# Batches 5 and 6 of a fused cross attention and SiLU network: the fourth half product in seven quarter products, with copies moved to ScalarE and an add moved on GpSimd

## Chip, cores and metric

One NeuronCore of a Trainium2 chip runs the kernel. The metric is the device time of one execution in microseconds (us); lower is better. Engines are named as in the profile: PE is TensorE (matrix products), PEld its weight loads, DVE is VectorE, ACT is ScalarE, POOL is GpSimd, SP is the queue of SyncE, which here issues most DMA transfers.

## What is computed

For each of 8 batches and 8 heads, x (512 tokens of 64) reads from a state of 32 rows by softmax attention, and the state reads from x. Both results are put side by side (544 rows a batch, 512 wide) and go through a two-layer network with SiLU.

```python
def _attn_ref(x, state):                      # x [8, 8, 512, 64], state [8, 8, 32, 64]
    scores = scale * np.matmul(x, state.transpose(0, 1, 3, 2))
    a = softmax(scores)
    xread = np.matmul(a, state)
    scores2 = scale * np.matmul(state, x.transpose(0, 1, 3, 2))
    a2 = softmax(scores2)
    sread = np.matmul(a2, x)
    return np.concatenate([xread, sread], axis=2)

def _moe_ref(x, w_in, w_out):                 # [4352, 512], [512, 2048], [2048, 512]
    h = x @ w_in
    g = h * (1.0 / (1.0 + np.exp(-h)))
    return g @ w_out
```

## The kernel before

**The tiling.** The tokens of a batch are one unit. For xread, `W1 = state @ w_in` is formed per batch in pieces of 512 columns (`w1_mms` on PE into PSUM, `w1_out` copying to bf16), so that h is `aT` times `W1`: `emit_G1(k)` does one block of 128 of the 2048 columns (L566, two matmuls of 128x512) and ScalarE applies SiLU (L594). The result g of a batch is kept in two tiles, `lo` (blocks 0 to 7) and `hi` (8 to 15). A ninth "batch" (number `B` = 8) is sread of all batches, with four matmuls a block (L584) from `xmT`.

**The second layer** is a product of 512 tokens by 2048 by 512, done from batch 1 on by a Strassen-Winograd scheme: seven half products (`Unit.mm(p, k)`, p from 1 to 7, L764), each of 256 tokens by 1024 by 256, that is 8 steps k of two matmuls of 128x256, in place of eight. Their operands are sums of parts of g (`sums1` to `sums4`, on VectorE) and of w_out (`D1` to `D4`). Two accumulators in PSUM are used: `al` (tag o1) collects products 1, 6 and 5, `be` (tag o0) takes 7, 2, 4 and 3 one after the other. What has to outlive an accumulator is copied to `kept[0]` (after product 1), `kept[1]` (product 7) or straight to the output tile (`keep`, after 6 and after 5).

**A half product in quarters.** `Split` does a half product by the same scheme once more: seven quarter products of four matmuls of 128x128 (L689), in the order 1, 2, 4, 7, 6, 3, 5. Its left sums are four VectorE operations (`sums`), its right sums `inner_weights`. Quarters 1, 6 and 5 add into one accumulator `o_ch`, in one of the four banks a0 to a3 that are handed out in turn by `bank`; the others have columns of `be`. VectorE copies `o_ch` to `kept` after 1 and again after 6, adds after 3, and copies and adds after 5. Before the change product 7 is so done in batches 2 to 7, and products 4 (`p4`) and 3 (`p3`) in batch 7.

**The order** is written out by hand: each engine does its instructions in the order in which the program issues them, and a semaphore wait stands where data or a buffer is shared. In batch b the loop over j emits the blocks of h of b and, between them, products 1 and 7 (`early`). After it come W1 pieces, scores and sread for later batches (`group_a`, `out_a`), product 2, product 6 (`units(6)`), `keep` on ScalarE, the add of `kept[1]` on GpSimd, product 4 (`units(4)`), further W1 pieces (`group_b`), product 5 and product 3. `units` puts blocks of h of the next batch between the steps where `leads` says so: none in product 4; in batch 7 the blocks of sread stand between the steps of products 6 to 3 (`upto`).

Other names: `exps_t(m)` is the exponential of the scores of batch m = b + 2 (two on ScalarE, with loads of the function table before and after, by the `warm` instructions) and a DMA transpose of it on SP; `norm_t` normalises it (VectorE and GpSimd). `sread_out` scales what the state read (VectorE) and `transpose_xm` transposes it by DMA; `place_xm(half, eng)` copies it into `xmT`, half 0 for batches 0 to 3. `last_weights` makes the right sums that `p4` (i from 0) and `p3` (from 4) need. `out_half` stores an output tile.

Of the kernel before, what the change touches and what calls it, by code (L numbers as in the profile page):

```python
# [9 lines left out]
BF16 = mybir.dt.bfloat16  # L10
# [8 lines left out]
B = 8  # L19
# [23 lines left out]
def kernel(  # L43
# [8 lines left out]
    nc = tc.nc  # L52
    ds = bass.ds
# [419 lines left out]
        for i, b in enumerate(bs):  # L473
            nc.sync.dma_start_transpose(xs[:, b, :], xm[:, i].rearrange("p g d -> p (g d)"))

    def place_xm(half, eng):
        src = xs.rearrange("p b (k o n) -> p b k o n", k=2, o=2)
        for hg in range(2):
            for odd in range(2):
                copy(  # L480
                    eng,
                    xmT[ds(64 * (odd ^ hg), 64), half, ds(2 * hg, 2), :, :],
                    src[ds(64 * hg, 64), ds(4 * half, 4), :, odd, :].rearrange(
                        "p b k n -> p k n b"
                    ),
                )
# [23 lines left out]
    def w1_out(b, cols, engs, pss, at=0):  # L510
        for f, n in cols:
            for hg in range(2):
                copy(engs[hg], W1[b][:, hg, ds(f + at, n)], pss[f, hg][:, ds(at, n)])
# [105 lines left out]
    def add(eng, dst, a, c):  # L619
        eng.tensor_tensor(dst, a, c, op=ADD)  # L620
# [29 lines left out]
    INNER = (2, 3, 4, 5, 6, 7)  # L650

    class Split:
        def __init__(self, unit, left, right, t, d, kept):
            self.unit, self.t, self.d, self.kept = unit, t, d, kept
            self.x, self.y = quarters(left), quarters(right)
            self.chain = None
            self.begun = set()
# [68 lines left out]
    class Unit:  # L726
# [53 lines left out]
                self.s2 = spool.tile([128, 8, 256], BF16, tag="s2", name="s2")  # L780
            sub(nc.vector, self.s2[:, k], self.hi[:, k, 256:512], self.lo[:, k, 256:512])

        def sums1(self):
            self.s1 = spool.tile([128, 8, 256], BF16, tag="s1", name="s1")
            for k0 in (0, 4):
                k = ds(k0, 4)
                add(nc.vector, self.s1[:, k], self.s2[:, k], self.lo[:, k, 0:256])

# [5 lines left out]
        def inner_sums(self, which):  # L794
            if self.inner is None:
                t = spool.tile([128, 4, 4, 128], BF16, tag="s1", name="inner")
                self.inner = Split(self, self.lo[:, :, ds(256, 256)], D3, t, wt2, self.kept[1])
            self.inner.sums(which)

        def block(self, i, c):  # L800
# [220 lines left out]
    def last_weights(i0, k):  # L1021
        for i in range(i0, i0 + k):
            w, d = divmod(i, 4)
            inner_weights(d, nc.vector, last_d[:, w], (D4, B22)[w])
# [6 lines left out]
    for b in range(1, B):  # L1031
# [2 lines left out]
        u = Unit(b)  # L1034
        lead = LEADS.get(b, 5)
        inner = b in INNER
        if b == 2:
            todo = [(1, k - 8, k + 4) for k in range(5)] + [(7, 1, 9)]
            todo += [(7, 2, 10), (7, 4, 10), (7, 7, 11), (7, 6, 12), (7, 3, 12), (7, 5, 13)]
            todo += [(1, k - 8, (k + 23) // 2) for k in range(5, 8)]  # L1040
        elif inner:
            todo = [(1, k - 8, k + 2) for k in range(6)] + [(7, 1, 9)]
            todo += [(7, 2, 10), (7, 4, 10), (7, 7, 11), (7, 6, 12), (7, 3, 13), (7, 5, 14)]
            todo += [(1, k - 8, 15) for k in (6, 7)]
        else:
            last = 6
            todo = [(1, k - 8, k + 2) for k in range(last)]
            todo += [(7, k - 8, k + 4) for k in range(8)]
            todo += [(1, k - 8, k + 2) for k in range(last, 8)]
        n_todo = len(todo)  # L1050

        def unit():
            p, k, _ = todo.pop(0)
            if k > 0:
                u.inner.mm(k)
                return
            u.mm(p, k + 8)
            if k == -1:
                copy(
                    nc.vector,  # L1060
                    u.kept[int(p == 7)][:],
                    (u.al if p == 1 else u.be)[:],
                )
# [9 lines left out]
        for j in range(lead, NFT):  # L1073
            upto(NFT * b + j + 1)
            if j == 8:
                u.hi = gh[b, 1]
            if j == max(lead, 5):
                u.sums3(0, 4)
                if b == 1:
                    transpose_x(3)  # L1080
                    for v in range(2):
                        evict_state(v, (nc.vector, nc.gpsimd)[v], 2, 2)
                if inner:
                    u.inner_sums((3,))
                if n > B - 2:
                    last_weights(4 * (n - B + 1), 2)
                if 1 < b and m + 1 < B:
                    fetch_x(m + 1)
            if j == 9:
                u.sums3(4, 4)  # L1090
                if inner:
                    u.inner_sums((1, 2, 4))
                if b == 1:
                    for i in range(4):
                        inner_weights(i, nc.vector)
                    spread_x(2)
                    for v in range(2):
                        evict_state(v, nc.gpsimd, 4, 4)
            if n > B - 2 and j == 12:
                last_weights(4 * (n - B + 1) + 2, 2)  # L1100
            early(j)
            if j == 13:
                u.sums2(0, 4)
                if b == 1:
                    fetch_x(4)
# [8 lines left out]

        def out_a():
            i, cols, engs, pss = made[0][0]
            w1_out(i, cols, (nc.scalar, nc.scalar) if b == 1 else engs, pss)
            xm = sread_out(srs, made[1]) if srs and m < B else None
            for piece in made[0][1:]:
                w1_out(*piece)  # L1120
            return xm

        while todo:
# [6 lines left out]
            u.sums1()  # L1130
        if 2 < b < B - 1:
            xm = out_a()
        if n == B:
            upto(NFT * B + 2)
            p4 = Split(u, u.hi[:, :, 256:512], D4, last_t[:, 0], last_d[:, 0], u.kept[0])
            p4.sums((3, 1, 2, 4))
        if b == 1:
            for hg in range(2):
                scores(2, hg)
# [5 lines left out]
            made = group_a()  # L1145
        add(nc.vector, u.block(0, 0), u.kept[0][:], u.be[:])
        if b > 1:
            u.sums1()
        if m == B:
            xm = sread_out(srs, made[1])  # L1150
        if b == 1:
            for hg in range(2):
                exps(2, hg)
# [2 lines left out]

        if b == 2:
            out_a()
        if 1 < b and m < B:
            exps_t(m)  # L1160
        if m == B:
            transpose_xm(srs, xm)
# [2 lines left out]
        def units(p, leads={}, split=None, into=None):  # L1165
            nonlocal step
            for k in range(8 if split is None else 7):
                if split is None:
                    u.mm(p, k)
                else:  # L1170
                    split.mm(ORDER[k], into)
                if n == B and (p != 6 or k > 5):
                    upto(NFT * B + 3 + (step + 1) * (NFT - 3) // 24)
                    step += 1
                    if (p, k) == (3, 1):
                        sread_diff()
                if n < B and k in leads:
                    upto(NFT * n + leads[k])

        units(6)  # L1180
        u.keep(nc.scalar, 1, 0)
        if b == 1:
            for hg in range(2):
                norm(2, hg)
        add(nc.gpsimd, u.block(1, 0), u.block(1, 0), u.kept[1][:])
        if b == 1:
            made = group_a()
            for c in range(4):
                cast_x(4, nc.gpsimd, c, 1)
            for hg in range(2):  # L1190
                transpose_a(2, hg)
            exps_t(m)
            transpose_x(4)
            xm = out_a()
        if m < B:
            nc.scalar.activation(warm[:], busy[:, 0:1], func=SILU, bias=0.0)
        if n < B:
            units(4)
            u.sums4()
            add(nc.vector, u.block(1, 0), u.block(1, 0), u.be[:])  # L1200
        else:
            units(4, split=p4)
            u.sums4()
            add(nc.vector, u.block(1, 0), u.block(1, 0), u.kept[0][:])
            p3 = Split(u, u.hi[:, :, 0:256], B22, last_t[:, 1], last_d[:, 1], u.kept[0])
            p3.sums((1, 2, 3, 4))
        def group_b():
            if b in PIECES_B:
                c = PIECES_B[b]
                pss = w1_next(2) + (w1_next(1, new_h) if c == 3 else [])  # L1210
                for i in (2, 0, 1)[3 - c :]:
                    if b == 1 and i == 1:
                        pss[i] = pss[i][:2] + ((nc.vector, nc.vector),) + pss[i][3:]
                    w1_out(*pss[i])

        if b > 1:
# [12 lines left out]
        else:  # L1229
            units(3, split=p3, into=u.block(0, 1))  # L1230
        if m == B:
            for half in range(2):
                place_xm(half, (nc.vector, nc.gpsimd)[half])
        if m < B:
            normed = norm_t(m)
        if n == B - 2:
            last_d, last_t = (
                xfpool.tile([128, 2, 4, 4, 128], BF16, tag=f"x_f{i}", name=nm)
                for i, nm in enumerate(("last_d", "last_t"))
            )  # L1240
# [46 lines left out]
```

## Time and profile before

| | us |
|---|---|
| median of three runs | 199.74 (199.67 to 199.80) |
| the profiled execution | 199.7 |
| its span | 197.9 |
| half products on PE (L764), busy | 46.6 + 27.4 + 14.4 |
| h on PE (L566, L584), busy | 72.8 + 9.4 |
| SiLU on ScalarE (L594), busy | 79.9 |
| GpSimd's adds to the output (L620), busy | 11.3 + 9.2 |

The span runs from the first to the last record of one execution; what lies around it makes up the rest of the time. The granted clock of PE was 0.996 of full speed over the span. Matmuls overlap: one of 128x256 shows 273 ns and one of 128x128 219 ns, from its start until its result is out, though the next one starts long before that. How long a run of matmuls holds PE is therefore read from the start of the run to the start of what follows.

By engine the busy share of the span is 97% on PE, 81% on VectorE, 70% on ScalarE and 37% on GpSimd. Batch 5's products 2 to 5 lie between 132.6 and 139.6 us, batch 6's between 152.8 and 160.5, batch 7's between 173.4 and 184.5; the last product ends at 194 us.

### The profile page before, as it was taken

What the parts mean: (1) busy time and instruction counts of PE and PEld (TensorE: products, weight loads), DVE (VectorE), ACT (ScalarE), POOL (GpSimd) and SP (SyncE); (2) the same over time, 40 slices, a digit from 0 to 9 for tenths busy, and PEclk for the clock granted to TensorE, in tenths of its full rate; (3) what the DMA queues carried; (4) which work ended last, traced back from release to release, by engine and by line L of the source; (5) the groups of instructions that cost most, each with busy time, mean ns of one, the idle gap of its engine ahead of it and who ended that gap; (6) DMA issues with size and microseconds to landing.
All of it is one profiled execution on the core that took longest, in us unless ns stands there. A gap on an engine that the chain in (4) does not pass through costs nothing.

```text
span 197.9 us, 4924 instructions
## 1 busy us (share of the span) xinstructions
PE 191.8 (97%) x2004; PEld 130.4 (66%) x2004; DVE 159.8 (81%) x314; ACT 138.8 (70%) x255; POOL 73.8 (37%) x97
## 2 busy tenths in 40 slices
PE   7899999999999999999999999999999999999992
PEld 2344455467766676667766776668766866699981
DVE  3755678999899799769994979779688998896782
ACT  3875496689779797889788967889588167825530
POOL 8595332895693008500850047102400236002220
PEclk9999999999999999999999999999999999999998
DMA  5999999999359462594239930942090005000043
GB/s 181 216 206 250 258 207 341 263 263 253 70 95 276 104 212 56 185 230 171 53 133 204 250 61 4 294 92 53 3 267 3 3 13 212 3 2 0 22 193 106
DMA packets 40838, 28.75 MB, mean 145 GB/s; under 512 B 27248, under 2 KB 37488, under 8 KB 40816
## 3 DMA queue, kind: packets, MB, share of 16 engines
q1 hardware_dynamic: 34736, 20.58, 39.8%
q0 software_dynamic: 5792, 7.60, 18.4%
q8 instruction: 15, 0.25, 0.5%
q10 hardware_dynamic: 288, 0.26, 0.4%
q14 instruction: 7, 0.06, 0.1%
HBM read 17.43 MB, written 8.91 MB: 133 GB/s over the span
## 4 chain that ended last, share of the span: by engine, by line
PE 94%; DMA 2%; DVE 1%; POOL 1%; ACT 0%; issue 0%; POOLq 0%
PE o L764 37%; PE h L566 28%; PE ps_w L499 4%; PE o L603 4%; PE o L689 4%; PE h L584 4%; PE o_a L603 3%; PE o_ch L689 3%; DMA x_f<-in_x_dram 2%; PE o_s L830 2%; PE o L830 1%; PE ps_sr L438 1%; PE ps_xt L261 1%; PE ps_at L420 1%; PE ps_sc L318 1%; PE ps_scT L344 1%
## 5 line engine op out<-in xcount | busy, mean ns | idle before, releaser
L594 ACT ACTIVATE g<-h 128x512 bf16<-128x512 f32 (+1 forms) x142 | 79.9, 573 | 29.0 <-PE h L566 17.5
L566 PE MATMUL h<-aT,W 128*128 128x512 bf16 x252 | 72.8, 379 | 0.0
L764 PEld LDWEIGHTS <-g 128*128 128x128 bf16 x432 | 41.7, 98 | 20.7 <-DVE kept L620 0.7
L764 PE MATMUL o<-w_out_sb,g 128*128 128x256 bf16 x320 | 46.6, 273 | 0.0
L620 POOL TENSOR_TENSOR o_sb<-o_sb,kept 128x512 f32<-128x512 f32 (+1 forms) x8 | 11.3, 1418 | 76.9 <-ACT o_sb L166 64.5
L566 PEld LDWEIGHTS <-W 128*128 128x128 bf16 x252 | 23.1, 98 | 7.0 <-issue 0.6
L764 PE MATMUL o<-wt,s 128*128 128x256 bf16 x224 | 27.4, 273 | 0.0
L168 DVE CAST W<-ps_w 128x512 bf16<-128x512 f32 (+1 forms) x34 | 21.2, 665 | 4.8 <-PE ps_w L499 4.8
L764 PEld LDWEIGHTS <-s 128*128 128x128 bf16 x224 | 21.5, 98 | 4.5 <-issue 2.1
L166 ACT ACTIVATE W<-ps_w 128x512 bf16<-128x512 f32 (+1 forms) x32 | 16.8, 582 | 7.5 <-PE ps_w L499 7.5
L168 POOL CAST x_nat<-x_f 128x512 bf16<-128x512 f32 x24 | 16.5, 728 | 3.3 <-DMA x_f<-in_x_dram 3.3
L166 ACT ACTIVATE o_sb<-o 128x512 f32<-128x512 f32 x15 | 8.9, 595 | 8.9 <-PE o L764 4.5
L620 POOL TENSOR_TENSOR o_sb<-kept,o_sb 128x512 f32<-128x512 f32 x7 | 9.2, 1307 | 15.3 <-ACT o_sb L166 15.3
L617 DVE TENSOR_TENSOR g<-g 128x1024 bf16<-128x1024 bf16 x15 | 10.8, 718 | 4.5 <-ACT g L594 4.5
L764 PE MATMUL o<-wt,g 128*128 128x256 bf16 x112 | 14.4, 273 | 0.0
L617 DVE TENSOR_TENSOR g<-g,s 128x1024 bf16<-128x1024 bf16 x14 | 14.2, 1058 | 0.0
L620 DVE TENSOR_TENSOR o_sb<-o_sb,o 128x512 f32<-128x512 f32 (+1 forms) x13 | 8.6, 661 | 3.6 <-PE o L764 2.0
L617 DVE TENSOR_TENSOR s<-g 128x512 bf16<-128x512 bf16 (+3 forms) x23 | 11.4, 523 | 0.0
L689 PEld LDWEIGHTS <-inner 128*128 128x128 bf16 x96 | 7.3, 98 | 5.4
L168 DVE COPY kept<-o_ch 128x128 f32<-128x128 f32 x16 | 4.6, 288 | 7.0 <-PE o_ch L689 6.9
L499 PE MATMUL ps_w<-w_in_sb,stT 64*32 64x512 bf16 (+1 forms) x264 | 10.2, 375 | 0.0
L603 PEld LDWEIGHTS <-g 128*128 128x128 bf16 x64 | 5.6, 98 | 6.4 <-issue 1.1
(143 smaller groups left out, 284.2 us busy)
## 6 DMA issues: line engine op xcount, KB each, us to landing
out_dram<-o_sb SPq DMA_DIRECT2D x14, 512.0 KB, 2.8
x_f<-in_x_dram SPq DMA_DIRECT2D x6, 512.0 KB, 4.5
w_out_sb<-in_moe_w_out_dram POOLq DMA_DIRECT2D x8, 256.0 KB, 9.8
x_f<-in_x_dram POOLq DMA_DIRECT2D x2, 1024.0 KB, 11.6
x_f<-in_x_dram SPq DMA_DIRECT2D x2, 1024.0 KB, 6.3
w_in_sb<-in_moe_w_in_dram POOLq DMA_DIRECT2D x3, 512.0 KB, 10.0
x_f<-in_x_dram POOLq DMA_DIRECT2D x2, 512.0 KB, 10.3
out_dram<-o_sb SPq DMA_DIRECT2D x4, 256.0 KB, 5.0
```

The source lines that it names most:

```text
L166: nc.scalar.activation(dst, src, func=COPY, bias=0.0)
L168: eng.tensor_copy(dst, src)
L499: nc.tensor.matmul(pss[f, hg][ds(32 * s, 32), 0:n], stT[ds(r, 64), b, h // 2, s % 2, :], w_in_sb[ds(r, 64), h // 2, ds(f, n)], start=True, ...
L566: nc.tensor.matmul(h_ps[k][:], W1[b][:, hg, ds(128 * ft, 128)], aT[b][:, hg, :, :], start=(hg == 0), stop=(hg == 1), skip_group_check=True,)
L584: nc.tensor.matmul(ps[:, 0:256], w_in_sb[:, kt, ds(128 * ft, 128)], xmT[:, :, kt].rearrange("p t n b -> p t (n b)"), start=(kt == 0), stop ...
L594: nc.scalar.activation(gt[k], ps[:, 0:n], func=SILU, bias=0.0)
L603: nc.tensor.matmul(outs[tt][:], gt[b * NFT + ft][:, ds(128 * tt, 128)], w_out_sb[:, ft, :], start=(ft == 0), stop=(ft == NFT - 1), skip_gr ...
L617: eng.tensor_tensor(dst, a, c, op=SUB)
L620: eng.tensor_tensor(dst, a, c, op=ADD)
L689: nc.tensor.matmul(to, left[:, k], right[:, k], start=where not in self.begun, stop=(k == 3), skip_group_check=True,)
L764: nc.tensor.matmul(to[:, t, :], left[:, ds(128 * t, 128)], right[:, k, :], start=first and t == 0, stop=(k == 7), skip_group_check=True,)
L830: nc.tensor.matmul(to[:, 0:n], left[:, k], right[:, k, ds(c, n)], start=(first and k == 0), stop=(k == 7), skip_group_check=True,)
```

## The change

In batches 5, 6 and 7 (`split`) product 4 is done in quarters; before, in batch 7 alone. Around it:

- `last_weights` runs in batches 5 and 6 (before: 6 and 7), and its tiles are taken after batch 4 (before: 5).
- In batches 5 and 6 ScalarE copies product 1 to `kept[0]` (before: VectorE).
- In batches 5 and 6 ScalarE does all copies of the W1 pieces of `out_a` (before: VectorE and ScalarE, half each). In `group_b` of batch 6 ScalarE copies the first piece, which now lies in the tag h1 of PSUM, and VectorE the second.
- `sread_out` of batch 6 comes ahead of product 2 (before: after it).
- In batches 5 to 7 `sums1` is cut in two: the second half is issued after the first quarter of product 4.
- In batch 5 `exps_t` comes after `keep` (before: ahead of product 6).
- In batches 2 to 7 GpSimd's add of `kept[1]` comes after VectorE's add of product 4 (before: ahead of product 4).
- `place_xm(0)` moves from the end of batch 6 into the loop of batch 7, in two parts.

```diff
-    def place_xm(half, eng):
+    def place_xm(half, eng, hgs=(0, 1)):
         src = xs.rearrange("p b (k o n) -> p b k o n", k=2, o=2)
-        for hg in range(2):
+        for hg in hgs:
...
-        def sums1(self):
-            self.s1 = spool.tile([128, 8, 256], BF16, tag="s1", name="s1")
-            for k0 in (0, 4):
+        def sums1(self, ks=(0, 4)):
+            if ks[0] == 0:
+                self.s1 = spool.tile([128, 8, 256], BF16, tag="s1", name="s1")
+            for k0 in ks:
...
+        split = b in (5, 6, 7)
...
                 copy(
-                    nc.vector,
+                    nc.scalar if b in (5, 6) else nc.vector,
                     u.kept[int(p == 7)][:],
...
-                if n > B - 2:
-                    last_weights(4 * (n - B + 1), 2)
+                if b in (5, 6):
+                    last_weights(4 * (b - 5), 2)
+                if n == B:
+                    place_xm(0, nc.vector, (0,))
...
-            if n > B - 2 and j == 12:
-                last_weights(4 * (n - B + 1) + 2, 2)
+            if b in (5, 6) and j == 12:
+                last_weights(4 * (b - 5) + 2, 2)
+            if n == B and j == 12:
+                place_xm(0, nc.vector, (1,))
...
-            w1_out(i, cols, (nc.scalar, nc.scalar) if b == 1 else engs, pss)
+            w1_out(i, cols, (nc.scalar, nc.scalar) if b == 1 or split else engs, pss)
             xm = sread_out(srs, made[1]) if srs and m < B else None
-            for piece in made[0][1:]:
-                w1_out(*piece)
+            for i, cols, engs, pss in made[0][1:]:
+                w1_out(i, cols, (nc.scalar, nc.scalar) if split else engs, pss)
...
+        if m == B:
+            xm = sread_out(srs, made[1])
+        if split:
+            p4 = Split(u.hi[:, :, 256:512], D4, last_t[:, 0], last_d[:, 0], u.kept[0])
+            p4.sums((3, 1, 2, 4))
         if n == B:
             upto(NFT * B + 2)
-            p4 = Split(u, u.hi[:, :, 256:512], D4, last_t[:, 0], last_d[:, 0], u.kept[0])
-            p4.sums((3, 1, 2, 4))
...
         if b > 1:
-            u.sums1()
-        if m == B:
-            xm = sread_out(srs, made[1])
+            u.sums1((0,) if split else (0, 4))
...
-        if 1 < b and m < B:
+        if 1 < b < 5:
             exps_t(m)
...
                     split.mm(ORDER[k], into)
+                    if (p, k) == (4, 0):
+                        u.sums1((4,))
...
         u.keep(nc.scalar, 1, 0)
+        if b == 5:
+            exps_t(m)
...
-        add(nc.gpsimd, u.block(1, 0), u.block(1, 0), u.kept[1][:])
         if b == 1:
+            add(nc.gpsimd, u.block(1, 0), u.block(1, 0), u.kept[1][:])
...
-        if n < B:
+        if split:
+            units(4, split=p4)
+            u.sums4()
+            add(nc.vector, u.block(1, 0), u.block(1, 0), u.kept[0][:])
+        else:
             units(4)
             u.sums4()
             add(nc.vector, u.block(1, 0), u.block(1, 0), u.be[:])
-        else:
-            units(4, split=p4)
-            u.sums4()
-            add(nc.vector, u.block(1, 0), u.block(1, 0), u.kept[0][:])
-            p3 = Split(u, u.hi[:, :, 0:256], B22, last_t[:, 1], last_d[:, 1], u.kept[0])
+        if b > 1:
+            add(nc.gpsimd, u.block(1, 0), u.block(1, 0), u.kept[1][:])
+        if n == B:
+            p3 = Split(u.hi[:, :, 0:256], B22, last_t[:, 1], last_d[:, 1], u.kept[0])
             p3.sums((1, 2, 3, 4))
...
-                pss = w1_next(2) + (w1_next(1, new_h) if c == 3 else [])
+                if m == B:
+                    pss = w1_next(1, new_h) + w1_next(1)
+                else:
+                    pss = w1_next(2) + w1_next(1, new_h)
                 for i in (2, 0, 1)[3 - c :]:
-                    if b == 1 and i == 1:
-                        pss[i] = pss[i][:2] + ((nc.vector, nc.vector),) + pss[i][3:]
+                    if b == 1 and i == 1 or m == B:
+                        eng = nc.scalar if m == B and i == 0 else nc.vector
+                        pss[i] = pss[i][:2] + ((eng, eng),) + pss[i][3:]
...
         if m == B:
-            for half in range(2):
-                place_xm(half, (nc.vector, nc.gpsimd)[half])
+            place_xm(1, nc.gpsimd)
...
-        if n == B - 2:
+        if b == 4:
             last_d, last_t = (
```

More of the change, by code (lines that the diff above doesn't have):

```diff
@@ L652, with __init__ @@
     class Split:
-        def __init__(self, unit, left, right, t, d, kept):
-            self.unit, self.t, self.d, self.kept = unit, t, d, kept
+        def __init__(self, left, right, t, d, kept):
+            self.t, self.d, self.kept = t, d, kept
             self.x, self.y = quarters(left), quarters(right)
@@ L796, in inner_sums @@
                 t = spool.tile([128, 4, 4, 128], BF16, tag="s1", name="inner")
-                self.inner = Split(self, self.lo[:, :, ds(256, 256)], D3, t, wt2, self.kept[1])
+                self.inner = Split(self.lo[:, :, ds(256, 256)], D3, t, wt2, self.kept[1])
             self.inner.sums(which)
```

## The prediction

> **What bounds the kernel now.** I read the busy times first, then the chain of waits, then the timelines of the engines around the fourth product in batches 5, 6 and 7. Busy time and chain:
>
> ```profile
> PE 191.8 (97%) x2004; PEld 130.4 (66%) x2004; DVE 159.8 (81%) x314; ACT 138.8 (70%) x255; POOL 73.8 (37%) x97
> ...
> PE 94%; DMA 2%; DVE 1%; POOL 1%; ACT 0%; issue 0%; POOLq 0%
> ```
>
> The end is set by TensorE (PE), which from about 17 us to the last product at 194 us is never idle. So what the other engines are spared is worth nothing by itself; only TensorE's own work and any wait that is put into its stream count. TensorE's timeline, batch 5 before (columns: start, length, then the instructions run together):
>
> ```profile
> 136.10 1.91 PE L764 MATMUL o<-wt,g 128*128 128x256 bf16 x16
> 137.85 1.91 PE L764 MATMUL o<-wt,s 128*128 128x256 bf16 x16
> ```
>
> These are the fourth and the fifth half product. From start to start a whole half product takes 137.85 − 136.10 = 1.75 us. Batch 7 already does its fourth product in quarters (in the order 1, 2, 4, 7, 6, 3, 5), with h products (L584) between:
>
> ```profile
> 177.72 0.39 PE L689 MATMUL o_ch<-wt,g 128*128 128x128 bf16 x4
> 177.94 0.39 PE L689 MATMUL o<-wt,g 128*128 128x128 bf16 x4
> 178.16 0.60 PE L584 MATMUL h<-xmT,w_in_sb 128*128 128x256 bf16 x4
> 178.60 0.39 PE L689 MATMUL o<-last_d,g 128*128 128x128 bf16 x4
> 178.82 0.39 PE L689 MATMUL o<-last_d,last_t 128*128 128x128 bf16 x4
> 179.04 0.60 PE L584 MATMUL h<-xmT,w_in_sb 128*128 128x256 bf16 x4
> 179.48 0.39 PE L689 MATMUL o_ch<-last_d,last_t 128*128 128x128 bf16 x4
> 179.71 0.39 PE L689 MATMUL o<-wt,last_t 128*128 128x128 bf16 x4
> 179.93 0.60 PE L584 MATMUL h<-xmT,w_in_sb 128*128 128x256 bf16 x4
> 180.37 0.39 PE L689 MATMUL o_ch<-last_d,last_t 128*128 128x128 bf16 x4
> ```
>
> **The quarters.** Without the h products the seven cost 0.44 + 0.44 + 0.45 + 0.22 (to 180.59) = 1.55 us, 28 matmuls of 55 ns. Each split thus takes 0.20 us of work off TensorE, and the two of batches 5 and 6 together 0.40 us. This is the whole gain that the change can have.
>
> **The wait that comes with them.** Products 1, 6 and 5 add into one accumulator, o_ch, which VectorE copies away after 1 and after 6; product 5 may not touch it until the copy after 6 is done. VectorE's timeline of the same batch 7 product:
>
> ```profile
> 179.91 0.29 DVE L168 COPY kept<-o_ch 128x128 f32<-128x128 f32 x1 [1.48 <-PE o_ch L689]
> 180.30 0.74 DVE L620 TENSOR_TENSOR kept<-kept,o 128x256 f32<-128x256 f32 x2
> ```
>
> Product 6 starts at 179.48 and is out at 179.87 (its 0.39), the copy begins 0.04 later and takes 0.29. To hand the accumulator back costs about 0.06 (the first transposed x was copied until 6.58, and TensorE went on at 6.64). That is 0.78 us from the start of 6 to the start of 5. In batch 7 it is covered: 6, 3 and an h product take 0.89. In batches 5 and 6 `units(4, split=p4)` has no leads, so nothing but product 3 lies between, and 6 and 3 take 0.44. TensorE waits 0.78 − 0.44 = 0.34 us in each batch, if VectorE is free when 6 ends. It is not quite: the second half of sums1 is now queued behind the copy after 1. Counted from the start of the fourth product, that copy runs from 0.43 to 0.71, the half sum (1.29/2 = 0.65) to about 1.36, while 6, begun at 0.89, is out at 1.28. That adds about 0.05 (0 to 0.15). The copy after 1 itself is done at 0.77 with its handing back, before 6 wants it at 0.89: no wait there.
>
> So the fourth product takes 1.55 + 0.34 + 0.05 = 1.94 us against 1.75: **+0.19 in each batch, +0.38 together**; bounds 1.89 to 2.05, so +0.28 to +0.60. What is queued behind the wait is everything on TensorE, the fifth product first.
>
> **Is the rest ready in time?** In batch 5's clock of before:
> - VectorE loses the copy of the first product (0.68) and two W1 casts (1.28) and gains four sums (1.6, as the same four in batch 7 from 174.34 to 175.93). It adds block(0,0) at about 134.65, as before at 134.80, does half of sums1 and is free at 135.95; the copy after product 1 is due at 136.53. In batch 6 sread_out comes ahead (0.17 + 0.42), and it is free some 0.4 us before. No wait.
> - ScalarE in batch 5: copy of the first product to 132.8, four W1 copies of 0.54 to 135.0, the table load (1.28) to 136.3, keep to 137.1. The fifth product needs the keep at 137.85 or later: 0.7 us of cover. Then two exps (1.15), a load (1.28), ready at 139.5, where the next h is out at 140.2 before: 0.7 us. The exps' transpose is issued some 2 us later, and norm_t with it; its aT is wanted a batch later, at 160.5.
> - After the split VectorE still has two adds, a copy and an add (1.45 as from 180.30 to 181.70), then sums4, the first half about 139.8; the third product starts past 140.2. Cover 0.4 us, thinner than before. This works because GpSimd's add has left sums4:
>
> ```profile
> 136.60 2.36 DVE L617 TENSOR_TENSOR g<-g,s 128x1024 bf16<-128x1024 bf16 x2
> ...
> 137.03 1.38 POOL L620 TENSOR_TENSOR o_sb<-o_sb,kept 128x512 f32<-128x512 f32 x1 [12.74 <-ACT o_sb L166]
> ...
> 181.62 1.28 DVE L617 TENSOR_TENSOR g<-g,s 128x1024 bf16<-128x1024 bf16 x2
> ```
>
> The same pair of sums takes 2.36 us beside that add (first two lines, batch 5) and 1.28 alone (last line, batch 7). The move saves VectorE 1.1 us in batches 2 to 6, worth nothing on the path. GpSimd's casts of x, block(1,1), its half of norm_t and SP's stores queue behind the add and start 1 to 2 us later in batches 2 to 5; what they feed is due most of a batch later. Zero, bounds −0.05 to +0.1 for all of them.
>
> **Batch 7** has half of xmT's placing moved into it, in place of last_weights (which batches 5 and 6 take on, with room as in batch 6 before). VectorE there:
>
> ```profile
> 169.63 0.41 DVE L617 TENSOR_TENSOR last_d<-w_out_sb 128x512 bf16<-128x512 bf16 x1
> 169.96 0.42 DVE L617 TENSOR_TENSOR last_d<-w_out_sb,last_d 128x512 bf16<-128x512 bf16 x1
> 170.50 0.29 DVE L168 COPY kept<-o_ch 128x128 f32<-128x128 f32 x1
> ```
>
> Two copies of 0.64 (four took 2.56 in batch 6) replace this pair of 0.75, +0.5 us; the earlier pair ran 1.2 us beside GpSimd's copies, and its successor takes 1.3 to 1.7. VectorE is 0.55 to 1.0 late at the copy after inner product 6: it ends at 171.2 to 171.6 with the handing back at 171.3 to 171.7, where product 5 is due at 171.38. Loss 0 to 0.3, and I take 0.1. GpSimd's add also comes later, beside the sums of p3 from 183.43 on. At the row for such a sum beside GpSimd (0.73 against 0.42) they end near 185.9 instead of 184.98, and the copy near 186.2, just before its product 6 at 186.28: nothing, or up to 0.2 if it slips.
>
> The Trainium skill, SBUF — State Buffer, section Who interferes with whom, says more: a VectorE operation with two inputs from SBUF and a GpSimd operation that reads SBUF lock each other out for a whole instruction. By it this slip would be up to one GpSimd add, some 1.3 us minus the slack, though the rows above show both engines working on, stretched.
>
> **Sum.** 0.38 + 0.1 = +0.48 us. The profiled execution is 199.7 (span 197.9 and 1.8 around it), the median 199.74: 199.74 + 0.48 = **200.2 us**.
>
> **Rivals.**
> 1. *Batch 7 becomes VectorE's*: the upper bounds there, +0.3 at 171 us and +0.2 at 186 us on top of 0.38, so 200.6. For it: VectorE has no gap between 171.15 and 177.8. Against: 0.36 us of idle time before the adds at 171.15 takes up part.
> 2. *The wait is mostly covered*: VectorE turns the copy round in 0.6 instead of 0.78, and both batches come out even with the 0.20 saved. 199.8. Against: 0.39 and 0.29 are rows.
> 3. *Product 5 does not wait*: the faster side, one mechanism at one place. If the hand-over of o_ch from 6 to 5 takes less than 0.44 us, all 0.40 is kept: 199.3. It decides from there on down; each 0.1 above takes 0.2 away over the two batches. Against: the matmul's 0.39 alone nearly fills it.
> 4. *Weights bind in a run of 28.* Weight loads are hidden in the runs so far; if each showed its whole 98 ns, 28 would take 2.74 us, +1.0 per batch: 201.7. Against: 16 in a row at 193.07 take 1.06 with the last one's drain of 0.22, or 56 ns apiece.
>
> The Trainium skill (TensorE: Matmul & The Clock Gate, Back-to-back issue gap) has such a rule against the change: matmuls of 128 columns, each with its own weight load, are sustained at about 81 ns. By it the quarters would take an estimated 28 × 0.081 = 2.27 us, more than the half product they replace; the run of 16 disagrees.
>
> **Chances.** Forecast (199.95 to 200.45) 0.52; rival 1 0.18; rival 2 0.13; rival 3 0.12; rival 4 0.05. 0.2% is 0.4 us, about what a measurement can tell from no change: 199.34 to 200.14 counts as the same. Of the forecast 0.30 lies above that and 0.22 within. Slower: 0.30 + 0.18 + 0.05 = 0.53; same 0.22 + 0.13 = 0.35; faster 0.12. The range 199.6 to 200.85 leaves out rivals 3 and 4 and nothing else of weight.
>
> **What would show it.** In batches 5 and 6: 28 matmuls at 55 ns; a gap on TensorE of some 0.35 to 0.4 us between products 3 and 5, released by VectorE's copy out of o_ch; the fifth product 1.9 to 2.0 us after the fourth. In batch 7 small gaps, if any, before inner product 5 and p3's 6. sums4 at 1.3 us. I am wrong if the gap is absent, or if TensorE gaps appear elsewhere: before the fifth product (keep) or the third (sums4).

## The result, and the profile after

The changed kernel takes 200.85 us (median of 6 runs, 200.72 to 201.15) against 199.70 before (6 runs, 199.53 to 200.0): a ratio of 1.0057, 95% interval 1.0044 to 1.0070. That is +1.15 us, slower, where +0.48 was forecast. The profiled execution took 200.84 with a span of 198.9, 1.0 more than before.

Busy time and chain of waits of the changed kernel, from its page:

```profile
PE 190.9 (96%) x2010; PEld 130.7 (66%) x2028; DVE 158.7 (80%) x328; ACT 141.4 (71%) x261; POOL 71.4 (36%) x97
...
PE 90%; DVE 6%; issue 1%; POOL 1%; ACT 0%; DVEq 0%; POOLq 0%
```

TensorE is busy 0.9 us less, and VectorE now has 6% of the chain: TensorE does less and waits for VectorE. The view of waits, TensorE alone, names the place (columns: total us, times, longest):

```profile
PE o_ch L689 <- DVE kept L168: 0.8, 3, 0.5
```

Three waits for the accumulator o_ch; before there was none. To see what each costs, the last third of the kernel is cut at five starts on TensorE that every kernel here has: the W1 matmuls of batch 5 (131.83 us before), those of batch 6 (151.65), batch 6's fifth product (158.73), the first run of `sread_out_product` (187.83) and its last (193.07). The lengths of the four stretches, in us, from the profiled executions:

| kernel | batch 5 | batch 6 | to the last product | last product | sum |
|---|---|---|---|---|---|
| before | 19.82 | 7.08 | 29.10 | 5.24 | 61.24 |
| changed | 19.96 | 7.22 | 29.78 | 5.34 | 62.30 |

So 0.14 is lost in each of batches 5 and 6, 0.68 in batch 7 and 0.10 behind it: 1.06 in all. The fourth product in batch 5, TensorE's timeline after:

```profile
136.04 0.39 PE L689 MATMUL o_ch<-wt,g 128*128 128x128 bf16 x4
...
136.94 0.39 PE L689 MATMUL o_ch<-last_d,last_t 128*128 128x128 bf16 x4
137.16 0.39 PE L689 MATMUL o<-wt,last_t 128*128 128x128 bf16 x4
137.71 0.38 PE L689 MATMUL o_ch<-last_d,last_t 128*128 128x128 bf16 x4 [0.16 <-DVE kept L168]
137.93 1.91 PE L764 MATMUL o<-wt,s 128*128 128x256 bf16 x16
```

The fifth product starts 137.93 − 136.04 = 1.89 us after the fourth, where it was 1.75. Between quarter 6 (136.94) and quarter 5 (137.71) lie 0.77 us, of which 6 and 3 fill 0.44: a wait of 0.33. (The profile shows 0.16 as idle, since it counts a matmul busy until its result is out.) Up to there the quarters run at (137.16 − 136.94)/4 = 55 ns a matmul.

The larger loss, in batch 7. TensorE after, in the quarters of `p3`:

```profile
186.53 0.39 PE L689 MATMUL o_ch<-last_d,last_t 128*128 128x128 bf16 x4
186.76 0.39 PE L689 MATMUL o<-w_out_sb,last_t 128*128 128x128 bf16 x4
186.98 0.60 PE L584 MATMUL h<-xmT,w_in_sb 128*128 128x256 bf16 x4
188.07 0.38 PE L689 MATMUL o_ch<-last_d,last_t 128*128 128x128 bf16 x4 [0.49 <-DVE kept L168]
```

Quarter 5 should start at 186.98 + 0.44 = 187.42 and starts at 188.07. VectorE and GpSimd in the same time:

```profile
183.64 0.42 DVE L620 TENSOR_TENSOR last_t<-g 128x512 bf16<-128x512 bf16 x1
184.09 1.38 DVE L617 TENSOR_TENSOR last_t<-last_t,g 128x512 bf16<-128x512 bf16 x1
185.39 0.41 DVE L617 TENSOR_TENSOR last_t<-g 128x512 bf16<-128x512 bf16 x1
185.73 0.41 DVE L617 TENSOR_TENSOR last_t<-g,last_t 128x512 bf16<-128x512 bf16 x1
186.06 0.28 DVE L168 COPY kept<-o_ch 128x128 f32<-128x128 f32 x1
186.26 1.55 DVE L617 TENSOR_TENSOR g<-g 128x1024 bf16<-128x1024 bf16 x1
187.74 0.28 DVE L168 COPY kept<-o_ch 128x128 f32<-128x128 f32 x1
```
```profile
183.86 1.32 POOL L620 TENSOR_TENSOR o_sb<-o_sb,kept 128x512 f32<-128x512 f32 x1 [16.87 <-DVE o_sb L620]
185.88 1.39 POOL L620 TENSOR_TENSOR o_sb<-kept,o_sb 128x512 f32<-128x512 f32 x1 [0.70 <-ACT o_sb L166]
```

The first GpSimd line is the add that was moved, the second the one that was always there. The second sum of `p3` (184.09) meets the moved add and takes 1.38 us instead of 0.42: it ends 0.3 us after the add, as if it had stood still until the add was over. All that follows is 1 us late. That reaches `sread_diff` (186.26). Before, it started ahead of the second add and kept its plain length, VectorE first, then GpSimd:

```profile
185.15 0.68 DVE L617 TENSOR_TENSOR g<-g 128x1024 bf16<-128x1024 bf16 x1
```
```profile
185.67 1.29 POOL L620 TENSOR_TENSOR o_sb<-kept,o_sb 128x512 f32<-128x512 f32 x1 [5.48 <-ACT o_sb L166]
```

Now it falls into that add and takes 1.55 instead of 0.68. The copy after quarter 6 (187.74) is queued behind it, and quarter 5 waits for the copy. A sum that had begun before an add started (183.64 and 185.73) keeps its length, and a copy out of PSUM (186.06) takes its usual 0.28 beside the second add.

The Trainium skill, SBUF — State Buffer, section Who interferes with whom, states this: a VectorE operation with two inputs from SBUF stands still while a GpSimd operation that reads SBUF holds the port. The prediction quoted that rule, but set it aside for rows that seemed to show both engines working on, stretched. The measurement decides for the page: 0.96 us of the sum's 1.38 and 0.87 of `sread_diff`'s 1.55 are such standing.

### The profile page after: what moved, and what is told of

Its sections match the earlier page's. It is cut to its first block, busy times and chain, and to the rows that moved or that the text cites. A ratio compares the mean times of both kernels' runs of the same rounds, so it can differ in the third digit from the quotient of the medians.

```text
span 198.9 us, 4980 instructions
## 1 busy us (share of the span) xinstructions
PE 190.9 (96%) x2010; PEld 130.7 (66%) x2028; DVE 158.7 (80%) x328; ACT 141.4 (71%) x261; POOL 71.4 (36%) x97
## 4 chain that ended last, share of the span: by engine, by line
PE 90%; DVE 6%; issue 1%; POOL 1%; ACT 0%; DVEq 0%; POOLq 0%
PE o L764 35%; PE h L566 26%; PE ps_w L499 4%; PE o L603 3%; PE o L689 3%; PE o_a L603 3%; PE o_ch L689 3%; PE ps_busy L174 2%; PE o_s L831 2%; PE h L584 2%; PE o L831 1%; DVE g L617 1%; PE ps_sr L438 1%; DVE last_t L617 1%; DVE kept L168 1%
## 5 line engine op out<-in xcount | busy, mean ns | idle before, releaser
L566 PE MATMUL h<-aT,W 128*128 128x512 bf16 x239 | 70.0, 379 | 0.1
L620 POOL TENSOR_TENSOR o_sb<-o_sb,kept 128x512 f32<-128x512 f32 (+1 forms) x8 | 10.0, 1255 | 95.1 <-DVE o_sb L620 93.3
L166 ACT ACTIVATE W<-ps_w 128x512 bf16<-128x512 f32 (+1 forms) x36 | 18.8, 590 | 7.1 <-PE ps_w L499 7.1
L168 DVE CAST W<-ps_w 128x512 bf16<-128x512 f32 (+1 forms) x30 | 18.6, 666 | 4.8 <-PE ps_w L499 4.7
L168 POOL CAST x_nat<-x_f 128x512 bf16<-128x512 f32 x24 | 15.3, 676 | 4.1 <-DMA x_f<-in_x_dram 4.1
L617 DVE TENSOR_TENSOR g<-g 128x1024 bf16<-128x1024 bf16 x15 | 12.3, 820 | 3.1 <-ACT g L594 3.0
L620 DVE TENSOR_TENSOR o_sb<-o_sb,o 128x512 f32<-128x512 f32 (+1 forms) x11 | 7.3, 661 | 6.5 <-PE o L764 5.7
L168 DVE COPY kept<-o_ch 128x128 f32<-128x128 f32 x20 | 5.8, 288 | 6.1 <-PE o_ch L689 6.1
L764 PE MATMUL o<-wt,g 128*128 128x256 bf16 x80 | 10.5, 273 | 0.1
L617 DVE TENSOR_TENSOR g<-g,s 128x1024 bf16<-128x1024 bf16 x14 | 10.0, 752 | 0.0
```

Source lines behind the costliest of these rows:

```text
L166: nc.scalar.activation(dst, src, func=COPY, bias=0.0)
L168: eng.tensor_copy(dst, src)
L566: nc.tensor.matmul(h_ps[k][:], W1[b][:, hg, ds(128 * ft, 128)], aT[b][:, hg, :, :], start=(hg == 0), stop=(hg == 1), skip_group_check=True,)
L617: eng.tensor_tensor(dst, a, c, op=SUB)
L764: nc.tensor.matmul(to[:, t, :], left[:, ds(128 * t, 128)], right[:, k, :], start=first and t == 0, stop=(k == 7), skip_group_check=True,)
```

## The experiments

Theory A: the loss is two waits for o_ch in batches 5 and 6, and in batch 7 GpSimd's moved add that locks VectorE. Theory B: VectorE is late in batch 7 for other reasons (the copies into xmT, the cut sums1). All kernels compute the whole result. Ratios are to the kernel before on the same chip, with 95% intervals.

**e1: the add back in its old place, in batch 7 only.** Against the changed kernel:

```diff
+        if b == B - 1:
+            add(nc.gpsimd, u.block(1, 0), u.block(1, 0), u.kept[1][:])   # ahead of units(4)
...
-        if b > 1:
+        if 1 < b < B - 1:
             add(nc.gpsimd, u.block(1, 0), u.block(1, 0), u.kept[1][:])
```

> The changed kernel with GpSimd's add of kept[1] put back ahead of the fourth product in batch 7 alone. Theory A (of the 1.15 us lost, two waits for the accumulator in batches 5 and 6 take 0.14 each, and GpSimd's add in batch 7, which locks VectorE out and makes p3 wait, takes 0.65 and another 0.1 in the last product): 200.85 - 0.75 = 200.1 us, and no gap on TensorE before p3's quarter 5. Theory B (VectorE is late in batch 7 because of the copies into xmT and the split sums1; the add's place does nothing): 200.85 us, the gap stays.

Measured 200.18 us, ratio 1.0016 (1.0007 to 1.0025), +0.32. The stretches are 19.96, 7.22, 29.09 and 5.24: the two waits of batches 5 and 6 remain, 0.28 together, and batch 7 costs nothing. VectorE's sums of p3 and sread_diff in e1:

```profile
184.23 0.42 DVE L617 TENSOR_TENSOR last_t<-last_t,g 128x512 bf16<-128x512 bf16 x1
...
185.50 0.68 DVE L617 TENSOR_TENSOR g<-g 128x1024 bf16<-128x1024 bf16 x1
```

Both have their plain length again. Theory B falls: its copies and its cut sums1 are all in e1.

**e2: the kernel before, with that one add moved.**

```diff
             add(nc.vector, u.block(1, 0), u.block(1, 0), u.kept[0][:])
+            add(nc.gpsimd, u.block(1, 0), u.block(1, 0), u.kept[1][:])   # batch 7; taken out ahead of units(4)
```

> The kernel before with nothing changed but GpSimd's add of kept[1] in batch 7, which comes after VectorE's add of product 4. Theory A: the whole of that loss without the rest of the change, 199.7 + 0.75 = 200.45 us. Theory B: 199.7 us.

Measured 200.60 us, ratio 1.0038 (1.0024 to 1.0051), +0.76. Stretches 19.83, 7.08, 29.77, 5.35: batch 7 and the last product as in the changed kernel, the rest as before. One instruction moved on an engine that is busy for 37% of the span costs two thirds of the whole loss. e1's +0.32 and e2's +0.76 add up to 1.08 of the 1.15.

**e3: the changed kernel, with sread_diff issued after the copy that it held up.**

```diff
-                    if (p, k) == (3, 1):
+                    if (p, k) == (3, 4):
                         sread_diff()
```

> The changed kernel with sread_diff issued after p3's quarter 6 and its copy, instead of after quarter 2. Theory A, in the form that the second GpSimd add holds sread_diff (1.55 us instead of 0.68) and the copy is queued behind it: the copy after quarter 6 is free of it, quarter 5 waits 0.1 us at most, and some 0.5 us come back: 200.35 us. If the late sums of p3 alone hold the copy: quarter 5 still waits 0.3 us or more, 200.6 us. Theory B: 200.85 us.

Measured 200.50 us, ratio 1.0034 (1.0021 to 1.0047), between the two sizes. The stretch of batch 7 is 29.13, so quarter 5 no longer waits, as the first form of theory A has it; but the last product takes 5.63 instead of 5.24. TensorE, ScalarE and GpSimd there:

```profile
190.48 1.03 PE L831 MATMUL o<-wt,s 128*128 128x256 bf16 x8 [0.23 <-ACT o_s L166]
```
```profile
190.04 0.38 ACT L166 ACTIVATE o_s<-o 128x256 f32<-128x256 f32 x1 [1.12 <-POOL o_sb L620]
```
```profile
188.89 1.12 POOL L620 TENSOR_TENSOR o_sb<-o_sb,kept 128x256 f32<-128x256 f32 x1 [1.36 <-DVE kept L620]
```

The adds after quarter 3 now stand behind sread_diff, GpSimd's third add starts later against TensorE, ScalarE may overwrite its buffer only then, and the product that uses the same accumulator waits. The lateness of VectorE was not cured, only passed on: +0.39 there. In the changed kernel the same run of the last product starts 0.12 late (190.59, after ScalarE's copy ends at 190.53), which accounts for the 0.10 lost there.

**e4: the wait filled.** e1, with a stretch of W1 matmuls between quarters 3 and 5 (the main lines):

```diff
...
+                    if k == 5 and fill is not None:
+                        fill()          # after quarter 3, in product 4
...
+            def fill():
+                if b == 5:
+                    filled.extend(w1_next(1))                        # 8 matmuls, taken out of group_a
+                else:
+                    filled.extend(w1_next(1, new_h) + w1_next(1))    # 16 matmuls, group_b's
...
```

> As e1, and in batches 5 and 6 one stretch of W1 matmuls (8 in batch 5, 16 in batch 6; both are in the changed kernel too, elsewhere) is issued between quarters 3 and 5 of the fourth product, where TensorE waits for the copy out of o_ch. Theory A: the waits of 0.34 us are filled with work that is due anyway, and the saving of 0.20 us in each batch shows: 199.7 - 0.40 = 199.3 us, up to 199.5 where 8 matmuls (0.28 us) don't fill the wait whole. If the quarters themselves are slower than 55 ns in a row of 28, or the wait isn't for the accumulator: 200.1 us, as e1.

Measured 199.87 us, ratio 0.9998 (0.9988 to 1.0009): better than e1 by 0.3 and level with before, but not 0.40 below it. Stretches 19.97, 6.91, 29.15, 5.24. Batch 6 does what theory A says: 0.17 less than before. TensorE in it:

```profile
157.50 0.39 PE L689 MATMUL o<-wt,last_t 128*128 128x128 bf16 x4
157.82 0.63 PE L499 MATMUL ps_w<-w_in_sb,stT 64*32 64x512 bf16 x16
158.38 0.40 PE L689 MATMUL o_ch<-last_d,last_t 128*128 128x128 bf16 x4
```

Quarter 5 follows the W1 matmuls without a wait. In batch 5 the filling did not pay: with the 8 small matmuls in it the fourth product took 2.01 us (135.89 to 137.90), 0.26 more than before, and without them group_a got only 0.11 shorter (from the last run of product 1 to product 2, 1.30 to 1.19). Between the quarters they held TensorE for 0.44 us, where 8 of them at the head of group_a take 0.22 (131.73 to 131.95). And the scores behind those took 0.44 instead of 0.33; the profile puts their late weight loads down to issue, and why is not shown.

**e5: batch 5 filled with a block of h instead**, the first one of the next batch; the 8 W1 matmuls go back to group_a. Against e4 (the main lines):

```diff
...
                 if b == 5:
-                    filled.extend(w1_next(1))
+                    upto(NFT * n + 1)
...
-        units(5, {7: 1} if b > 1 else {})
+        units(5, {7: 2 if b == 5 else 1} if b > 1 else {})
```

> As e4, but in batch 5 the gap between quarters 3 and 5 is filled with the first block of the next batch's h (two matmuls of 128x512, 0.43 us, which the changed kernel issues behind the fifth product) instead of 8 W1 matmuls; the second block then comes behind the fifth product. Theory A, with the rows of e4 (batch 6 took 6.91 us where it took 7.08 before, batch 5 took 6.17 where it took 6.02, because small W1 matmuls in a stretch of their own cost some 0.2 us of change-over): batch 5 now keeps its 0.2 us too, both together 0.37 below the kernel before, a ratio of 0.9982 and about 199.45 us. If the fill in batch 5 fails for another reason (the h buffers held by the scores, the third product waiting for sums4): no better than e4, 199.85 us.

Measured 199.63 us, ratio 0.9999 (0.9990 to 1.0008): a miss. Stretches 19.81, 6.91, 29.15, 5.24. TensorE and ScalarE in batch 5:

```profile
137.38 0.39 PE L689 MATMUL o<-wt,last_t 128*128 128x128 bf16 x4
137.74 0.38 PE L566 MATMUL h<-aT,W 128*128 128x512 bf16 x1
138.17 0.39 PE L689 MATMUL o_ch<-last_d,last_t 128*128 128x128 bf16 x4
```
```profile
137.48 0.20 ACT L358 ACTIVATION_READ_ACCUMULATOR eT<-ps_scT 128x1 f32 x1
```

The block starts 0.14 late, 0.06 after ScalarE is done with the scores in the h buffer. The fourth product takes 2.13 us with the block in it (136.26 to 138.39) and 1.70 without the block's 0.43: 0.05 less than before, where 0.2 was expected. So the late start is most of what batch 5 lacks. The rest of the miss, −0.13 by the stretches against −0.02 measured, is within the interval.

**e6: the kernel before, with the add moved in batches 2 to 6**, the same edit as e2 in the other batches.

> The kernel before with GpSimd's add of kept[1] moved behind VectorE's add in batches 2 to 6 and not in 7. Theory A: no wait on TensorE hangs on it there, 199.8 us (ratio 0.9995 to 1.0005), though sums4 takes 1.3 us in these batches instead of up to 2.4. If the add's move costs something in every batch: five times what is lost in none of the kernels yet, 200.2 us or more.

Measured 199.78 us, ratio 1.0003 (0.9991 to 1.0016); stretches 19.82, 7.08, 29.10 and 5.24, each as before. There the move is free, as predicted.

**e7: e5, with exps_t of batch 5 back ahead of product 6**, so that the buffer is free in time.

> As e5, with exps_t of batch 5 back ahead of the sixth product. In e5 the filling block of h started 0.14 us late (137.74 instead of 137.60), when the first exp had given its h buffer back. If that buffer was what ate the saving in batch 5, the block starts at once, batch 5's stretch from its W1 matmuls to batch 6's falls from 19.81 to 19.67 us, batch 6's stays at 6.91, and the kernel comes out 0.2 to 0.3 us below the one before: ratio 0.9985 to 0.9990, 199.4 us. If the keep, which now stands behind the exps, holds the fifth product, or something else eats it: ratio 1.0000.

Measured 199.50 us, ratio 0.9990 (0.9980 to 0.9999): at the upper end of what was expected, but not in the way expected. By the stretches e7 is no faster than e5, and the intervals of the two ratios overlap. The block of h starts at once, and the fourth product is 0.18 shorter than before, yet the stretch stays at 19.81. VectorE, GpSimd, and the weight loads of TensorE, in e7:

```profile
142.80 1.63 DVE L381 TENSOR_TENSOR an<-e,rcn 128x512 bf16<-128x512 bf16 x1
...
144.95 0.93 DVE L617 TENSOR_TENSOR g<-g 128x1024 bf16<-128x1024 bf16 x1
```
```profile
142.61 1.26 POOL L620 TENSOR_TENSOR o_sb<-kept,o_sb 128x512 f32<-128x512 f32 x1
143.83 1.50 POOL L381 TENSOR_TENSOR an<-e,rcn 128x512 bf16<-128x512 bf16 x1
```
```profile
147.79 0.45 PEld L689 LDWEIGHTS <-g 128*128 128x128 bf16 x8 [0.45 <-DVE g L617]
```

TensorE waits until 147.79 for VectorE's sums3. VectorE comes late to norm_t (142.80, before 141.10), since the split has given it more to do (copies and adds from 138.04 to 139.44), and there norm_t's product takes 1.63 us (0.69 in batch 5 before) and the first sums3 0.93. Each meets one of the two GpSimd instructions shown and ends some 0.55 us after it. If the late add has pushed these two there, moving it back will show it. What is free in e6 is not free once TensorE comes sooner.

**e8: e7, with the add early in batches 5 and 6 too.**

```diff
-        if b == B - 1:
+        if split:
             add(nc.gpsimd, u.block(1, 0), u.block(1, 0), u.kept[1][:])   # ahead of units(4)
...
-        if 1 < b < B - 1:
+        if 1 < b < 5:
```

> As e7, with GpSimd's add of kept[1] ahead of the fourth product in batches 5 and 6 too (so in all batches that split it; behind it only in 2 to 4). In e7 batch 5's stretch stayed at 19.81 us although its fourth product was 0.18 shorter: TensorE waited at 147.79 for sums3, and VectorE was 0.8 us late there, since norm_t's product took 1.63 us instead of 0.69 and the first sums3 0.93 instead of 0.69, each beside an instruction of GpSimd's. If the late add is behind this (it pushes GpSimd's later two instructions onto them), the stretch falls to 19.65 us, batch 7's 29.15 to 29.10, and the kernel stands at a ratio of 0.9983, 199.4 us. If it isn't: as e7, 0.9990.

Measured 199.45 us against 199.99 before on that chip, ratio 0.9979 (0.9968 to 0.9989): faster than both kernels. Stretches 19.64, 6.91, 29.09 and 5.24, so 0.18 and 0.17 below before in batches 5 and 6, and nothing lost elsewhere. The late add was behind the wait. VectorE's product of norm_t in e8, beside a GpSimd add that now ends at 142.91:

```profile
142.57 0.89 DVE L381 TENSOR_TENSOR an<-e,rcn 128x512 bf16<-128x512 bf16 x1
```

The first sums3 still takes 0.93, but starts at 143.98 instead of 144.95, and TensorE no longer waits for sums3.

The stretches of all kernels, with their sums and the measured ratios:

| kernel | batch 5 | batch 6 | to the last product | last product | sum less before's | ratio |
|---|---|---|---|---|---|---|
| changed | 19.96 | 7.22 | 29.78 | 5.34 | +1.06 | 1.0057 |
| e1 | 19.96 | 7.22 | 29.09 | 5.24 | +0.27 | 1.0016 |
| e2 | 19.83 | 7.08 | 29.77 | 5.35 | +0.79 | 1.0038 |
| e3 | 19.97 | 7.21 | 29.13 | 5.63 | +0.70 | 1.0034 |
| e4 | 19.97 | 6.91 | 29.15 | 5.24 | +0.03 | 0.9998 |
| e5 | 19.81 | 6.91 | 29.15 | 5.24 | −0.13 | 0.9999 |
| e6 | 19.82 | 7.08 | 29.10 | 5.24 | 0.00 | 1.0003 |
| e7 | 19.81 | 6.91 | 29.15 | 5.24 | −0.13 | 0.9990 |
| e8 | 19.64 | 6.91 | 29.09 | 5.24 | −0.36 | 0.9979 |

One profiled execution and the timed runs agree within some 0.1 us, or 0.05%, throughout.

## Why the prediction was right, and where it was not

**Right: the direction, and the mechanism in batches 5 and 6.** The hand-over of o_ch from quarter 6 to quarter 5 was put at 0.78 us and took 0.77; the quarters were put at 55 ns a matmul and took 55 to 56. The fourth product was put at 1.94 us and took 1.89. The 0.05 too much was for the half of sums1 queued ahead of the copy: it ended at 137.36, when quarter 6 came out (136.94 + 0.39 = 137.33). e4's batch 6 (0.17 below before) and e8 (0.18 and 0.17) show that the saving of some 0.2 us a batch is there once the wait is filled; in batch 5 the exps and the add had to go back to their old places as well.

**Right: the keep, sums4 and the moves in batches 2 to 6** cost nothing in the changed kernel (e6 for the add). e7 and e8 show that batch 5's late add would have cost 0.17 as soon as the wait was gone.

**Wrong in size: GpSimd's add in batch 7.** The prediction has the place, in its sum (nothing, or up to 0.2 if it slips) and in rival 1, but not the price, which is 0.76 by e2.
- The step that failed: it followed the lateness to the copy after quarter 1, found that it just fits, and stopped there. It does fit: quarter 6 did not wait for that copy. But next in VectorE's queue was sread_diff, which the lateness pushed into the second add, and the copy after quarter 6 was queued behind it.
- The price under it was wrong too, and by luck this did not show up to there. It priced a sum beside GpSimd at 0.73 against 0.42, from a row beside a short copy of GpSimd's, so that p3's sums were to end 0.9 late. In the run one of them took 1.38 and the others their plain length, and the last ended 0.95 late (186.14 against 184.98 before, less the 0.21 by which TensorE itself was later). The price is not a factor; it is what is left of GpSimd's instruction, up to 1.3 us for an add.

**The number is partly luck.** 200.85 is the last figure of the range (199.6 to 200.85), above the forecast's 199.95 to 200.45 and above rival 1's 200.6. The upper bounds of all three terms at once, 0.60 + 0.3 + 0.2, would give 200.84, but the loss was not made like that: the first two came out at their lower bounds, and the third was 0.76. By its own sign, a gap on TensorE elsewhere, the prediction failed in batch 7: it looked for small gaps before inner product 5 and p3's 6, and one of 0.65 came before p3's 5.

The evidence was in the profile of before, hidden in means. Its groups for sums4 and for VectorE's copies into xmT, one line each (columns: shortest, median and longest in ns):

```profile
L617 DVE TENSOR_TENSOR g<-g,s x14: 681/685/1758, 54.0 to 182.2; 128x1024 bf16<-128x1024 bf16 x14
```
```profile
L168 DVE COPY xmT<-xs x4: 358/378/1407, 161.2 to 162.4; 64x256 bf16<-64x256 bf16 x4
```

The pair of sums4 that took 2.36 us, which the prediction read as both engines working on, stretched, was one sum of about 0.7 and one that stood through GpSimd's add. The copies that it read as 0.64 each were three of less than 0.4 and one of 1.41.

**Wrong, to the other side: batch 7 at 171 us.** The 0.1 (0 to 0.3) for the copies into xmT was nothing: the pair at 169.95 took 0.77 where 1.28 was reckoned, for the same reason, and the stretch from batch 6's fifth product to batch 7's second (158.95 to 173.56, before 158.73 to 173.35) is 14.61 against 14.62.

The four terms as predicted and found: the fourth product 0.38, found 0.28; batch 7 at 171 us 0.1, found 0; p3 and the last product 0 to 0.2, found 0.76 to 0.78; the moves in batches 2 to 6 nothing, found nothing.

**The other rivals.** The wait was neither mostly covered nor absent (2 and 3). Weights did not bind (4): 20 matmuls with a weight load each, from 136.04 to 137.16, took 56 ns apiece. The Trainium skill's figure of some 81 ns (TensorE: Matmul & The Clock Gate, Back-to-back issue gap) is not what this run shows.

## What to carry to other kernels

A product cut into smaller ones that share an accumulator saves its time only if something stands between the last write and the next use of it: reckon the hand-over (result out, copy, semaphore; here 0.77 us) and put work that is due anyway into it, of the same tile shape or a whole stretch of another (e4's 16 matmuls paid, its 8 did not). Before an instruction of GpSimd's is moved, list every VectorE instruction with two inputs from SBUF that can start while it runs (and copies from SBUF to SBUF: the one of 1.41 us above met an add), price each at what is left of GpSimd's instruction, and follow the lateness through VectorE's queue to the next meeting. Read the shortest and longest of a group, not its mean: an instruction that stands still now and then looks like one that is always slow.

## What was not expected of the hardware

VectorE's port behaviour is all or nothing. A sum with both inputs in SBUF whose turn came while a GpSimd add ran took 1.38 us instead of 0.42, one that had begun before such an add kept its 0.41, and a copy out of PSUM beside one kept its 0.28. Held-up sums whose plain length is 0.68 ended 0.54 to 0.56 us after GpSimd's instruction, however long they had stood (sread_diff in the changed kernel, norm_t's product and sums3 in e7 and e8).

And a stretch of W1 matmuls, which work on 64x32 tiles, between quarters costs TensorE about 0.1 us at each end. In e4's batch 6, 0.10 us pass before the first (157.50 + 0.22 = 157.72 to 157.82), and the 16 take 0.56 until quarter 5, where 16 take 0.44 when the scores follow in the same tile shape (131.83 to 132.27 before).
